# A fused attention and GEGLU block: all engines in written order in the FFN, attention in eight pieces, LayerNorm sums from the residual add and a Square

## The chip, the cores and the metric

The kernel runs on one core of a Trainium2 chip. The metric is the device time of one execution in microseconds (us). Every figure for a kernel is the median of several executions unless it is said to be of one profiled execution; the span in a profile is some 1.7 us shorter than the time of the same execution. A run is called slow when it is over 1.5% above the fastest of the same kernel; one execution of one experiment was, and it is left out. The granted clock is the share of TensorE's full clock that the profile records; at 0.50, half clock.

Names of engines in the profile: PE is TensorE (matmul), PEld its weight loads, DVE VectorE, ACT ScalarE, POOL GpSimd, SP SyncE, which issues most transfers. An L with a number is a line of that kernel's own text, so the same statement has slightly different numbers in different kernels.

## The reference

2048 tokens of width 640, bf16; 32 heads of width 20; FFN width 1536.

```python
def _A_ref(x, wqkv, w_phi, wo):            # linear attention, H = 32, Dh = 20
    q, k, v = ...                          # x @ wqkv, split into heads
    pq = jnp.einsum("bhsd,hdf->bhsf", q, w_phi)
    pk = jnp.einsum("bhsd,hdf->bhsf", k, w_phi)
    phi_q = jnp.concatenate([_softmax(pq), _softmax(-pq)], axis=-1)
    phi_k = jnp.concatenate([_softmax(pk), _softmax(-pk)], axis=-1)
    kv = jnp.einsum("bhsf,bhsd->bhfd", phi_k, v)
    z = jnp.einsum("bhsf->bhf", phi_k)
    num = jnp.einsum("bhqf,bhfd->bhqd", phi_q, kv)
    den = jnp.einsum("bhqf,bhf->bhq", phi_q, z)[..., None] + 1e-6
    return merge_heads(num / den) @ wo     # (shortened)

def _B_ref(x, w_gate, w_up, w_down):
    return (_gelu(x @ w_gate) * (x @ w_up)) @ w_down

h  = x + _A_ref(_layernorm(x), A_wqkv, A_w_phi, A_wo)
h2 = h + _B_ref(_layernorm(h), B_w_gate, B_w_up, B_w_down)
```

## The kernel before

It has three stages. *Statistics*: for each of 16 tiles of 128 tokens LN1, a transpose, the value and key projections (pv, pk; w_phi is folded into the key and query weights beforehand), and the sums kvp. *Queries*: the query projection pq of all tiles, and attention of the first tiles. *FFN*: gate and up projection (gu), gelu, product GT, down projection (pd); attention of the later tiles is woven between these units. A unit of the FFN is one gate_up or one down call. Cut to what the change and the argument touch:

```python
    ctx.enter_context(tc.manual_schedule(engines={nc.tensor.engine, nc.sync.engine}))   # written order, to the end
    man_cm = tc.manual_schedule()                 # written order on all engines ...
    man_cm.__enter__()
    ...
    def ln_stats(pool, tiles, tag, act=True):
        ...
            for i in range(2):
                nc.vector.bn_stats(stats[:, i, :], xt[:, i * HD:(i + 1) * HD])
            nc.vector.bn_aggr(mv[:, j, :], stats)
        nc.gpsimd.tensor_scalar_add(ve, mv[:, :, 1], EPS)
        nc.gpsimd.tensor_tensor(rstd, ve, nhalf[:, 0:n], op=ALU.pow)
        if act:
            nc.gpsimd.tensor_tensor(mr, mv[:, :, 0], rstd, op=ALU.mult)
            nc.gpsimd.tensor_scalar_mul(mr, mr, -1.0)
    ...
    for t in range(NT):                           # statistics
        k_tile(t)
        ...
        if t == 12:
            fold(WqT, Wq2)                        # casts of wa: alternately ScalarE and VectorE
        if t + 3 < NT:
            v_tile(t + 3)
        if 6 <= t + 5 < NT:
            ln_ap(t + 5, on_act=True)             # normalise on ScalarE, then transpose by DMA
        k_norm(t)                                 # sk, rs on VectorE; vt on GpSimd and VectorE
        if t % 2 == 1 and t + 7 < NT:
            ln_st(t + 7, t + 8)                   # LN1 statistics
        if t % 2 == 1 and t >= 5:
            kv_tile(t - 5)
            kv_tile(t - 4)
    ...
    def attn_a(t): ...                            # ab matmuls, AB on ScalarE
    def attn_b(t):                                # pr, den, rd: VectorE
        ...
    def attn_b2(t, on_pe=False):                  # w, tt, o: VectorE; transpose of o by DMA
        ...
    def attn_c(t): ...                            # po matmuls
    def attn_d(t, act=True):                      # residual add, LN2 statistics
        ht = x_sb[t // 4][:, t % 4, :]
        h2 = ht.rearrange("p (u f) -> p u f", u=2)
        nc.vector.tensor_tensor(h2, st[t][:, :, 0:HD], h2, ALU.add)
        st[t] = ln_stats(p2, [ht], "2", act)[0]
    def attn_e(t): ...                            # LN2 applied on ScalarE, transpose by DMA
    ...
    man_cm.__exit__(None, None, None)             # ... until here; the scheduler orders DVE, ACT, POOL from now on

    def attn_at(t, i, start=0, slow=2, sep=0):    # at which unit which piece is written
        pcs = [(i, attn_a, t), (i + 1, attn_b, t), (i + 1 + sep, attn_b2, t),
               (i + 3 + slow, attn_c, t), (i + 4 + slow, attn_d, t), (i + 5 + slow, attn_e, t)]
        ...
    weave(gus(0, 0, 256) + downs(0, (0, 1)), ...)           # first pass, half-width units
    weave(gus(0, 256, 512) + downs(0, (2, 3)), ...)         # second
    for b in range(1, NB):                                  # blocks 1, 2, 3
        ...
```

The softmax here doesn't subtract the row's maximum and nothing guards it: scores larger than these inputs give would overflow.

## Time and profile before

| | before |
|---|---|
| time, median of the first 3 executions | 297.85 us (296.56 to 298.58) |
| span of the profiled execution | 298.0 us |
| TensorE busy | 94% |
| VectorE, ScalarE, GpSimd busy | 64%, 45%, 26% |
| stretch from first pk to first gu | 84.3 us |
| stretch from first gu to last pd matmul | 192.8 us |

The last two rows are differences of start times in the timeline of TensorE. As TensorE is busy almost throughout, such a stretch is its work plus its stops, and it doesn't move with what happened before it.

### The profile page before, as it was taken

Reading aid. Unit: us, or ns where it says so; the run is one execution under the profiler, and the core shown is the slowest. Engines: PE = TensorE matmul, PEld = TensorE weight load, DVE = VectorE, ACT = ScalarE, POOL = GpSimd, SP = SyncE. Lnnn points to the kernel's source line nnn. Section 1 sums busy time; section 2 is a strip of 40 time slices with the busy share of each in tenths; the row PEclk is TensorE's granted clock in tenths of the full one; section 3 lists DMA queues with packets and bytes.
Section 4 is the critical chain, followed back from the end, with each engine's and each line's share of the span. In section 5 each row is a group of like instructions: output and inputs, shape, how many; then the busy total and the mean of one; then the engine's idle time right before and its main releaser. Section 6 shows DMA issues by size and latency. Waiting matters only on the chain.

```text
span 298.0 us, 5561 instructions
## 1 busy us (share of the span) xinstructions
PE 280.7 (94%) x2233; PEld 179.8 (60%) x2233; DVE 189.7 (64%) x370; ACT 133.0 (45%) x200; POOL 77.7 (26%) x138
## 2 busy tenths in 40 slices
PE   6799699989999899799999998999998999999995
PEld 2576477765555678477876554577554567544473
DVE  4799979878276599574755868643777753232322
ACT  1479768866968846234242443410534321122200
POOL 5439877855221101311110033110002321000000
PEclk9999989999999999989999999999999999999999
DMA  7995312381080021513112112221111422100011
GB/s 216 263 343 167 54 23 50 65 311 66 2 264 2 0 25 34 56 45 77 35 25 66 23 24 46 44 60 52 46 22 22 45 46 68 44 0 0 2 41 47
DMA packets 40968, 21.01 MB, mean 71 GB/s; under 512 B 33136, under 2 KB 39280, under 8 KB 40944
## 3 DMA queue, kind: packets, MB, share of 16 engines
q1 hardware_dynamic: 39712, 19.50, 26.6%
q10 hardware_dynamic: 1232, 1.17, 1.2%
q8 instruction: 17, 0.28, 0.4%
q14 instruction: 7, 0.06, 0.1%
HBM read 10.18 MB, written 2.62 MB: 43 GB/s over the span
## 4 chain that ended last, share of the span: by engine, by line
PE 69%; DVE 9%; issue 8%; POOL 6%; DMA 4%; ACT 3%; ACTq 0%; POOLq 0%
PE gu L479 28%; PE pd L494 15%; PE pq L309 7%; PE pk L236 5%; PE po L459 5%; PE pv L236 4%; DVE stats L100 3%; PE ab L408 2%; PE kvp L281 2%; POOL rstd L105 2%; POOL vt L270 1%; DMA LN1T<-ln 1%; DMA x_sb<-in_A_x_dram 1%; DMA oT<-o 1%; DVE x_sb L467 1%
## 5 line engine op out<-in xcount | busy, mean ns | idle before, releaser
L479 PE MATMUL gu<-LN2T,Wg 128*128 128x512 bf16 (+1 forms) x300 | 61.7, 336 | 2.1 <-DVE GT L485 1.5
L479 PE MATMUL gu<-LN2T,Wu 128*128 128x512 bf16 (+1 forms) x300 | 61.7, 336 | 0.0
L485 DVE TENSOR_TENSOR GT<-gu,g 128x512 bf16<-128x512 f32 (+1 forms) x60 | 34.2, 577 | 38.2 <-ACT g L482 38.1
L482 ACT ACTIVATE g<-gu 128x512 bf16<-128x512 f32 (+1 forms) x60 | 29.5, 507 | 59.0 <-PE gu L479 57.5
L494 PE MATMUL pd<-Wd,GT 128*128 128x320 bf16 x384 | 53.6, 299 | 2.1 <-DVE GT L485 2.1
L494 PEld LDWEIGHTS <-GT 128*128 128x128 bf16 x384 | 37.5, 98 | 17.3 <-DVE GT L485 2.9
L103 POOL TENSOR_SCALAR ve<-mv 128x1 f32<-128x1 f32 (+1 forms) x26 | 5.9, 226 | 145.1 <-DVE mv L101 140.1
L479 PEld LDWEIGHTS <-Wg 128*128 128x128 bf16 x300 | 29.0, 98 | 23.2 <-issue 2.7
L479 PEld LDWEIGHTS <-Wu 128*128 128x128 bf16 x300 | 29.3, 98 | 22.6
L236 PEld LDWEIGHTS <-LN1T 128*128 128x128 bf16 x320 | 30.9, 99 | 15.8 <-DMA LN1T<-ln 3.3
L115 ACT ACTIVATE ln<-x_sb,mr,rstd 128x640 bf16<-128x640 bf16 x24 | 22.2, 923 | 37.4 <-POOL mr L110 37.4
L270 POOL TENSOR_TENSOR vt<-vS,rs 128x672 bf16<-128x672 bf16 x22 | 32.9, 1507 | 13.1 <-DVE rs L267 13.1
L500 DVE TENSOR_TENSOR y<-pd,x_sb 128x640 bf16<-128x640 f32 (+1 forms) x17 | 13.3, 782 | 30.2 <-PE pd L494 30.2
L100 DVE BATCH_NORM_STATS2 stats<-x_sb 128x6 f32<-128x320 bf16 x64 | 27.7, 474 | 2.6 <-DMA x_sb<-in_A_x_dram 2.1
L236 PE MATMUL pv<-Wv,LN1T 128*128 128x320 bf16 x160 | 25.1, 306 | 2.8 <-DMA LN1T<-ln 2.4
L413 ACT COPY AB<-ab 128x968 f32<-128x968 f32 x16 | 15.4, 966 | 25.9 <-PE ab L408 25.9
L459 PE MATMUL po<-Wo,oT 128*128 128x320 bf16 x160 | 25.5, 308 | 0.7 <-DVE GT L485 0.4
L265 DVE TENSOR_REDUCE sk<-E 128x64 f32<-128x1280 bf16 x16 | 23.6, 1472 | 3.4 <-ACT E L259 3.4
L440 DVE TENSOR_TENSOR tt<-AB,w 128x1280 bf16<-128x1280 f32 x16 | 23.9, 1492 | 0.6
L236 PE MATMUL pk<-Wk,LN1T 128*128 128x320 bf16 x160 | 24.2, 299 | 0.0
L259 ACT ACTIVATE E<-pk 128x640 bf16<-128x640 f32 x32 | 20.7, 703 | 7.0 <-PE pk L236 7.0
L309 PE MATMUL pq<-LN1T,Wq 128*128 128x512 bf16 x100 | 22.9, 379 | 0.4 <-ACT Eq L314 0.4
(63 smaller groups left out, 258.3 us busy)
## 6 DMA issues: line engine op xcount, KB each, us to landing
out_dram<-y SPq DMA_DIRECT2D x15, 160.0 KB, 1.8
Wg<-in_B_w_gate_dram SPq DMA_DIRECT2D x1, 1920.0 KB, 11.8
Wu<-in_B_w_up_dram SPq DMA_DIRECT2D x1, 1920.0 KB, 9.3
Wd<-in_B_w_down_dram SPq DMA_DIRECT2D x1, 1920.0 KB, 8.0
x_sb<-in_A_x_dram SPq DMA_DIRECT2D x2, 640.0 KB, 5.5
Wv<-in_A_wqkv_dram SPq DMA_DIRECT2D x2, 400.0 KB, 5.8
Wo<-in_A_wo_dram SPq DMA_DIRECT2D x1, 800.0 KB, 5.1
x_sb<-in_A_x_dram ACTq DMA_DIRECT2D x1, 640.0 KB, 6.8
```

The source lines that it names most:

```text
L100: nc.vector.bn_stats(stats[:, i, :], xt[:, i * HD:(i + 1) * HD])
L115: nc.scalar.activation(ln, xt, ACTF.Identity, bias=mr, scale=rstd)
L236: nc.tensor.matmul(ps[:, u, 0:HD], lhsT=lnT(t, c), rhs=W[:, c, u * HD:(u + 1) * HD], start=(c == 0), stop=(c == NC - 1))
L265: nc.vector.reduce_sum(sk, Ek[t].rearrange("p s (h f) -> p (s h) f", f=Dh), axis=AX.X)
L270: eng.tensor_tensor(vt[:, s], vS[t % 6], rs[:, s * H:(s + 1) * H, None].to_broadcast([P, H, VC]), ALU.mult)
L309: nc.tensor.matmul(pqs[j][:, i, :], lhsT=Wq2[:, kc, c * P:(c + 1) * P], rhs=LN1T[b][:, kc, :], start=(kc == 0), stop=(kc == NC - 1))
L440: nc.vector.tensor_tensor(tt.rearrange("p s (h f) -> p s h f", f=Dh), num, w[:, :, :, None].to_broadcast([P, 2, H, Dh]), ALU.mult)
L459: nc.tensor.matmul(po[:, u, 0:HD], lhsT=st[t][:, c, :], rhs=Wo[:, c, u * HD:(u + 1) * HD], start=(c == 0), stop=(c == NC - 1))
L479: nc.tensor.matmul(gu[:, i, 0:n], lhsT=W[:, c, f * P:(f + 1) * P], rhs=LN2T[b][:, c, a0:a1], start=(c == 0), stop=(c == NC - 1))
L482: nc.scalar.activation(g[:, 0:n], gu[:, 0, 0:n], ACTF.Gelu_apprx_tanh)
L485: nc.vector.tensor_tensor(st[b, "g", f][:, a0:a1], gu[:, 1, 0:n], g[:, 0:n], ALU.mult)
L494: nc.tensor.matmul(pd[:, u, 0:HD], lhsT=st[b, "g", f][:, tl * P:(tl + 1) * P], rhs=Wd[:, f, u * HD:(u + 1) * HD], start=(f == 0), stop=(f ...
```

## The change

Four intents. (1) In the FFN, too, VectorE, ScalarE and GpSimd follow the written order, and attention is cut into eight pieces at new offsets, so that no piece stands ahead of work that is ready. (2) VectorE is relieved: small products of attention go to GpSimd, and LN2's mean and variance come from the residual add's accumulator and a Square on ScalarE in place of bn_stats. (3) At the start and in the statistics the LN1 work is moved up. (4) Loads are reordered and output stores issued three units later. The diff, cut to its core (cuts marked with an ellipsis):

```diff
@@ ln_stats, small operation @@
-            nc.gpsimd.tensor_tensor(mr, mv[:, :, 0], rstd, op=ALU.mult)
-            nc.gpsimd.tensor_scalar_mul(mr, mr, -1.0)
+            for j in range(n):
+                nc.gpsimd.tensor_scalar(mr[:, j:j + 1], mv[:, j, 0:1], rstd[:, j:j + 1], -1.0, ...)
@@ loads: first tiles of x and w_phi change places and queues @@
+    nc.scalar.dma_start(wphi, ...)
     nc.sync.dma_start(x_sb[0][:, 0:1, :], x_v[:, 0:1, :])
-    nc.scalar.dma_start(x_sb[0][:, 1:2, :], x_v[:, 1:2, :])
+    nc.sync.dma_start(x_sb[0][:, 1:2, :], x_v[:, 1:2, :])
...
@@ start: third tile's statistics earlier, mask product BD from GpSimd to VectorE @@
+    ln_st(2, act=False)
     ln_ap(1, on_pe=True)
...
-    nc.gpsimd.tensor_tensor(BD, ...)
...
+    nc.vector.tensor_tensor(BD, ...)
@@ statistics @@
-        k_norm(t)
         if t % 2 == 1 and t + 7 < NT:
             ln_st(t + 7, t + 8)
+        k_norm(t)
@@ attention: b, b2, b3 (pr, den | rd, w | tt, o); eng is GpSimd in the FFN @@
-        nc.vector.tensor_tensor(pr, ...)
+        eng.tensor_tensor(pr, ...)
...
@@ attn_d, and a new attn_d2 @@
+        nc.vector.scalar_tensor_tensor(h2, st[t][:, :, 0:HD], 1.0, h2, op0=ALU.mult, op1=ALU.add, accum_out=sm[:, 0:1])
...
+        nc.scalar.activation(sq, ht, ACTF.Square, accum_out=sm[:, 1:2])
+        ...                                      # four one-column operations and a pow on GpSimd: rstd and -mean*rstd
@@ FFN @@
-    man_cm.__exit__(None, None, None)            # before the FFN
+    SHORT = (0, 2, 3, 4, 9, 9, 10, 12)           # offsets of the eight pieces, in units
+    LONG = (0, 1, 2, 3, 6, 6, 7, 8)
...
+    man_cm.__exit__(None, None, None)            # after it
```

More of the change, by code (lines that the diff above doesn't have):

```diff
@@ L108, in ln_stats @@
         if act:
-            nc.gpsimd.tensor_tensor(mr, mv[:, :, 0], rstd, op=ALU.mult)
-            nc.gpsimd.tensor_scalar_mul(mr, mr, -1.0)
+            for j in range(n):
+                nc.gpsimd.tensor_scalar(mr[:, j:j + 1], mv[:, j, 0:1], rstd[:, j:j + 1], -1.0,
+                                        op0=ALU.mult, op1=ALU.mult)
         return [(xt, mv[:, j, 0:1], rstd[:, j:j + 1], mr[:, j:j + 1]) for j, xt in enumerate(tiles)]
@@ L147 @@
     WqT = p1.tile([P, NC, D], BF16, name="WqT")
+    nc.scalar.dma_start(wphi, phi_v.rearrange("(c p) f -> p c f", p=P))
     nc.sync.dma_start(x_sb[0][:, 0:1, :], x_v[:, 0:1, :])
-    nc.scalar.dma_start(x_sb[0][:, 1:2, :], x_v[:, 1:2, :])
+    nc.sync.dma_start(x_sb[0][:, 1:2, :], x_v[:, 1:2, :])
     for u in range(2):
         nc.sync.dma_start(Wv[:, :, u * HD:(u + 1) * HD], w_v[:, :, 2 * D + u * HD:2 * D + (u + 1) * HD])
-        if u == 0:
-            nc.scalar.dma_start(x_sb[0][:, 2:3, :], x_v[:, 2:3, :])
-            nc.scalar.dma_start(wphi, phi_v.rearrange("(c p) f -> p c f", p=P))
-    nc.scalar.dma_start(x_sb[0][:, 3:4, :], x_v[:, 3:4, :])
+        nc.scalar.dma_start(x_sb[0][:, 2 + u:3 + u, :], x_v[:, 2 + u:3 + u, :])
     nc.sync.dma_start_transpose(WkT, A_wqkv[:, D:2 * D])
@@ L323 @@
     warm(2)
-    ln_st(2, act=False)
-    nc.gpsimd.tensor_tensor(BD, wphi[:, :, None, :].to_broadcast([P, NC, 8, Dh]),
-                            hmask[:, :, :, None].to_broadcast([P, NC, 8, Dh]), ALU.mult)
     v_mm(0, (0,))
@@ L335 @@
     v_ev(1)
+    nc.vector.tensor_tensor(BD, wphi[:, :, None, :].to_broadcast([P, NC, 8, Dh]),
+                            hmask[:, :, :, None].to_broadcast([P, NC, 8, Dh]), ALU.mult)
     ln_st(3, act=False)
@@ L419, in attn_a, with attn_b, attn_b2, attn_b3 @@
         st[t] = AB
-    def attn_b(t):
+    def attn_b(t, on_pe=False):
+        eng = nc.vector if on_pe else nc.gpsimd
         AB = st[t]
         pr = small(p2, [P, H, 2], "pr", 2)
-        nc.vector.tensor_tensor(pr, AB[:, 0, :, Dh:KC], AB[:, 1, :, 0:KC:KC - 1], ALU.mult)
+        eng.tensor_tensor(pr, AB[:, 0, :, Dh:KC], AB[:, 1, :, 0:KC:KC - 1], ALU.mult)
         den = small(p2, [P, H], "den", 2)
-        nc.vector.tensor_tensor(den, pr[:, :, 0], pr[:, :, 1], ALU.add)
+        eng.tensor_tensor(den, pr[:, :, 0], pr[:, :, 1], ALU.add)
+        st[t] = AB, den
+    def attn_b2(t, on_pe=False):
+        eng = nc.vector if on_pe else nc.gpsimd
+        AB, den = st[t]
         rd = small(p2, [P, H], "rd", 2)
         nc.vector.reciprocal(rd, den)
-        st[t] = AB, rd
-    def attn_b2(t, on_pe=False):
-        AB, rd = st[t]
         w = small(p2, [P, 2, H], "w", 2)
         for s in range(2):
-            nc.vector.tensor_tensor(w[:, s], AB[:, 1 - s, :, s * (KC - 1)], rd, ALU.mult)
+            eng.tensor_tensor(w[:, s], AB[:, 1 - s, :, s * (KC - 1)], rd, ALU.mult)
+        st[t] = AB, w
+    def attn_b3(t, on_pe=False):
+        AB, w = st[t]
         tt = p2.tile([P, 2, D], BF16, name="tt", bufs=2)
@@ L466, in attn_d, with attn_d2 @@
         h2 = ht.rearrange("p (u f) -> p u f", u=2)
-        nc.vector.tensor_tensor(h2, st[t][:, :, 0:HD], h2, ALU.add)
-        st[t] = ln_stats(p2, [ht], "2", act)[0]
+        if not act:
+            nc.vector.tensor_tensor(h2, st[t][:, :, 0:HD], h2, ALU.add)
+            st[t] = ln_stats(p2, [ht], "2", False)[0]
+            return
+        sm = small(p2, [P, 2], "sm", 2)
+        nc.vector.scalar_tensor_tensor(h2, st[t][:, :, 0:HD], 1.0, h2, op0=ALU.mult, op1=ALU.add, accum_out=sm[:, 0:1])
+        st[t] = sm
+    def attn_d2(t):
+        sm = st[t]
+        ht = x_sb[t // 4][:, t % 4, :]
+        sq = p2.tile([P, D], BF16, name="sq", bufs=1)
+        nc.scalar.activation(sq, ht, ACTF.Square, accum_out=sm[:, 1:2])
+        v = small(p2, [P, 3], "v2", 2)
+        nc.gpsimd.tensor_scalar(v[:, 0:1], sm[:, 0:1], sm[:, 0:1], -1.0 / (D * D), op0=ALU.mult, op1=ALU.mult)
+        nc.gpsimd.tensor_scalar_add(v[:, 0:1], v[:, 0:1], EPS)
+        nc.gpsimd.tensor_scalar(v[:, 1:2], sm[:, 1:2], 1.0 / D, v[:, 0:1], op0=ALU.mult, op1=ALU.add)
+        rstd = small(p2, [P, 1], "rstd2")
+        nc.gpsimd.tensor_tensor(rstd, v[:, 1:2], nhalf[:, 0:1], op=ALU.pow)
+        nc.gpsimd.tensor_scalar(v[:, 2:3], sm[:, 0:1], rstd, -1.0 / D, op0=ALU.mult, op1=ALU.mult)
+        st[t] = ht, None, rstd, v[:, 2:3]
     def attn_e(t, on_pe=False, on_dve=False):
@@ L488, in down @@
         if u == 0:
-            st["pd"] = gtile("pd"), p2.tile([P, D], BF16, name="y", bufs=3)
+            st["pd"] = gtile("pd"), p2.tile([P, D], BF16, name="y", bufs=4)
         pd, y = st["pd"]
@@ L501, in down, with store @@
                                     x_sb[b][:, tl, :].rearrange("p (u f) -> p u f", u=2)[:, a:u + 1], ALU.add)
-            nc.sync.dma_start(o_v[:, 4 * b + tl, a * HD:(u + 1) * HD], y[:, a * HD:(u + 1) * HD])
-    later = []
+            stores.append((lag, o_v[:, 4 * b + tl, a * HD:(u + 1) * HD], y[:, a * HD:(u + 1) * HD]))
+            if b == NB - 1 and tl >= 2:
+                store(lag)
+    later, stores, lag = [], [], 3
+    def store(n):
+        stores[:] = [(i - n, *x) for i, *x in stores]
+        while stores and stores[0][0] <= 0:
+            _, dst, src = stores.pop(0)
+            nc.sync.dma_start(dst, src)
     def weave(units, stages):
@@ L513, in weave @@
                 g(*a)
+            store(1)
             fn(*args)
@@ L527 @@
     q_mm(q + 1)
-    attn_b(0)
+    attn_b(0, True)
     attn_b2(0, True)
+    attn_b3(0, True)
     attn_a(1, True)
@@ L535 @@
     q_mm(q + 3)
-    attn_b(1)
+    attn_b(1, True)
     attn_b2(1, True)
+    attn_b3(1, True)
     attn_c(0)
@@ L552, with attn_at @@
     attn_e(1, True, True)
-    man_cm.__exit__(None, None, None)
     assert q + 6 == len(Eq)
-    def attn_at(t, i, start=0, slow=2, sep=0):
-        pcs = [(i, attn_a, t), (i + 1, attn_b, t), (i + 1 + sep, attn_b2, t), (i + 3 + slow, attn_c, t), (i + 4 + slow, attn_d, t), (i + 5 + slow, attn_e, t)]
-        return pcs if start == 0 else pcs[start:]
+    def attn_at(t, i, offs):
+        fns = (attn_a, attn_b, attn_b2, attn_b3, attn_c, attn_d, attn_d2, attn_e)
+        return [(i + o, fn, t) for fn, o in zip(fns, offs) if o >= 0]
+    SHORT = (0, 2, 3, 4, 9, 9, 10, 12)
+    LONG = (0, 1, 2, 3, 6, 6, 7, 8)
     weave(gus(0, 0, 256) + downs(0, (0, 1)),
-          attn_at(2, 0, 1, 3, 1) + attn_at(3, 3, 0, 3, 1) + attn_at(4, 6, 0, 4) + attn_at(5, 9, 0, 4) + attn_at(6, 13, 0, 4))
-    weave(gus(0, 256, 512) + downs(0, (2, 3)), attn_at(7, 3, 0, 4))
+          attn_at(2, 0, (-1, 0, 1, 2, 7, 7, 8, 10)) + attn_at(3, 1, SHORT) + attn_at(4, 6, SHORT) + attn_at(5, 9, SHORT) +
+          attn_at(6, 13, SHORT))
+    weave(gus(0, 256, 512) + downs(0, (2, 3)), attn_at(7, 2, SHORT))
     for b in range(1, NB):
@@ L568 @@
             for tl in range(4):
-                stages += attn_at(4 * b + 4 + tl, (0, 2, 5, 7)[tl])
+                stages += attn_at(4 * b + 4 + tl, (0, 2, 5, 7)[tl], LONG)
         weave(gus(b, 0, 512) + downs(b, range(4)), stages)
+    man_cm.__exit__(None, None, None)
 _INS = ['A_x', 'A_wqkv', 'A_w_phi', 'A_wo', 'B_x', 'B_w_gate', 'B_w_up', 'B_w_down']
```

## The prediction

> **What bounds the kernel now.** I read the page first, then the chain of waits, then the timeline of TensorE, then all engines around each hole in it.
>
> ```profile
> PE 280.7 (94%) x2233; PEld 179.8 (60%) x2233; DVE 189.7 (64%) x370; ACT 133.0 (45%) x200; POOL 77.7 (26%) x138
> ...
> PEclk9999989999999999989999999999999999999999
> ```
>
> TensorE is the bound in every stage; VectorE is dense only in the first 60 us. The second line shows two dents in the granted clock. How fast TensorE can go is read from the chain, where nothing else interferes:
>
> ```profile
> 194.59 13.04 PE pd L494 x96
> ...
> 255.92 25.90 PE gu L479 x120
> ```
>
> That is 0.136 us for 320 columns and 0.216 us for 512, start to start. With such a floor for every width (columns at 2.4 GHz plus 2.5 ns; 0.022 us for the half-array matmuls that make kvp) I summed over the whole timeline the distance from each start to the next less the floor. Floor 270.0 us, lost 23.4 us, first start at 1.25 us, 3.36 us after the last start: together 298.0. The change removes no matmul, so it can only win inside the 23.4. By stretch: 0 to 20 us 6.3; 20 to 40 us 4.6; 40 to 100 us 2.3 (mostly the query fold at 61 to 63 us); 100 to 132 us 6.7; 140 to 150 us 1.0; around 180 us 1.1; around 228 us 1.1. The big ones:
>
> ```profile
> 11.66 0.45 PE L128 MATMUL tp<-ident,ln 128*128 128x128 bf16 x5 [1.43 <-DVE ln L120]
> ...
> 36.08 2.39 PE L236 MATMUL pv<-Wv,LN1T 128*128 128x320 bf16 x10 [2.41 <-DMA LN1T<-ln]
> ```
>
> Behind the first: a GpSimd mask product and a VectorE normalisation that start together, the latter then taking 1.64 us where its neighbours take 0.45:
>
> ```profile
> 9.89 1.52 POOL L326 TENSOR_TENSOR BD<-wphi,hmask 128x800 bf16<-128x800 bf16 x1
> 9.97 1.64 DVE L120 TENSOR_SCALAR ln<-x_sb,mv,rstd 128x640 bf16<-128x640 bf16 x1 [1.00 <-POOL rstd L105]
> ```
>
> Behind the second: GpSimd does two vt products before the small LayerNorm operations that ScalarE needs:
>
> ```profile
> 26.52 2.59 POOL L270 TENSOR_TENSOR vt<-vS,rs 128x672 bf16<-128x672 bf16 x2
> 29.20 0.22 POOL L103 TENSOR_SCALAR ve<-mv 128x2 f32<-128x2 f32 x1
> ...
> 30.86 0.92 ACT L115 ACTIVATE ln<-x_sb,mr,rstd 128x640 bf16<-128x640 bf16 x1 [0.49 <-POOL mr L110]
> ```
>
> The hole in the first FFN pass, all engines:
>
> ```profile
> 120.95 1.49 DVE L440 TENSOR_TENSOR tt<-AB,w 128x1280 bf16<-128x1280 f32 x1
> ...
> 121.03 1.50 POOL L110 TENSOR_SCALAR mr<-mr 128x1 f32<-128x1 f32 x1
> 121.09 1.52 PE L494 MATMUL pd<-Wd,GT 128*128 128x320 bf16 x10
> 122.57 0.92 ACT L115 ACTIVATE ln<-x_sb,mr,rstd 128x640 bf16<-128x640 bf16 x1 [3.08 <-POOL mr L110]
> 123.39 0.64 ACT L482 ACTIVATE g<-gu 128x256 bf16<-128x256 f32 x2
> ...
> 124.27 0.31 PE L494 MATMUL pd<-Wd,GT 128*128 128x320 bf16 x1 [1.66 <-DVE GT L485]
> ```
>
> The scheduler put the normalisation on ScalarE ahead of two gelus whose inputs were ready; it waits for a one-column GpSimd operation that takes 1.50 us instead of 0.24 because tt runs; TensorE waits for the gelus. The same triple (tt, mr of 1.41 us, ln ahead of gelu) stands at 176 to 178 us and again 48 us later.
>
> Both long holes are followed by half clock:
>
> ```profile
> 36.58:40.00 3.42, 3.42 (x49) 2.28 (x48) 3.32 (x5) 1.45 (x2) 2.50 (x3) 0.50 0.00 0
> ...
> 125.33:128.75 3.42, 3.42 (x23) 2.35 (x22) 0.84 (x2) 0.00 (x0) 0.00 (x0) 0.50 0.50 96
> ```
>
> **What the Trainium skill says.** (1) "TensorE: Matmul & The Clock Gate", section "What's actually happening": the gate judges a free-running window of 3413 ns and halves the clock after an idle one. The trace agrees on the length, not on "idle": both windows before were still about a third busy. The hole at 9.9 to 11.7 us cost no clock. (2) The same page, "Wait - 56ns, not 53.3ns?": N / 2.4 GHz plus 2.5 ns per matmul; the chain rows agree (135.8 and 215.8 ns). (3) "SBUF — State Buffer", "Who interferes with whom": a VectorE instruction with two SBUF inputs, or in a two-port mode, and a GpSimd one that reads SBUF exclude each other for a whole instruction. Agreed: 1.50 against 0.24, 1.64 against 0.45. (4) "ScalarE: Activation LUTs", "What ACT_TABLE_LOAD costs": an ACTIVATE with immediates is 186 ns + 0.833 ns a column, and a switch of table costs a load (1.28 us here, twice in the kernel). Square on 640 columns: 0.72 us by that; the 640-column PSUM copies here take 0.70.
>
> **The change part by part.**
>
> *Start.* The mask product goes to VectorE (800 elements; the 672-element product there takes 0.86, so about 1.0 us) behind the third tile's normalisation, whose statistics move up. By hand from the durations: second tile's transpose 0.4 us later; third tile's statistics end near 7.9, rstd near 8.8, its normalisation at 9.3; TensorE reaches its transpose at 10.4 without a stop, against 11.66. The key fold then meets WkT, which landed at 13.4 us, and VectorE's copies of it come about a microsecond earlier. First key projection 16.5 instead of 17.6: **-1.0**. The reordered loads keep the first tile first; I count nothing for them.
>
> *Statistics before k_norm.* On GpSimd the rstd and mr of tiles 8, 9 end near 28.5 instead of 30.8, so ln of tile 8 becomes limited by ScalarE's own order, 0.6 us earlier. The transpose then took 4.2 us where most take 2.6, with an instruction fetch of 1.2 us on one DMA engine inside it. Without a collision the stop of 2.57 almost vanishes, with one about 1.8 stay. I take **-1.5**. VectorE falls further behind on k_norm, but kvp takes those four to five tiles later. Half clock behind it: 10 matmuls lose 0.13 each, about 1.4; at three in four that it goes, **-1.1**.
>
> *Work moved off VectorE.* For each of 14 tiles pr 0.23, den 0.19, w 0.35, two statistics 0.89, aggregate 0.21: 1.9 us, 26 us in all. Added: Square on ScalarE, 14 x 0.72 = 10 us (45% busy); on GpSimd four operations on 32 to 64 columns (0.25 to 0.3 by its 84-column rows at 0.33) and four one-column ones plus the power 0.57: about 2.5 us a tile in place of 1.25. All of it is beside TensorE; it counts through order only.
>
> *Written order, first pass.* Lost there: 0.54 + 0.12 + 0.43 + 0.18 + 1.82 + 0.60 and 1.05 of half clock = 4.7. By hand with the new offsets: the table load delays the first gelu as now, so with tile 3's attn_a at unit 1, unit 2 waits 0.35 for a PSUM buffer; tt and o of tiles 2 and 3 come before GT of units 2 and 5 on VectorE, so the first po waits about 1.1 for GT of unit 5; 0.15 elsewhere. The last gelu now comes before a Square, not behind a blocked ln: GT 11 lands just as the down projection asks for it. New loss 1.6: **-3.1**.
>
> *Second half-pass and blocks 1, 2.* Lost 0.59 + 0.43, then 1.1 twice. With 2.16 us units and ln emitted a unit after its GpSimd chain, I find no stop; I leave 0.2 in each: **-0.8** and **-1.8**. The late stores only keep transposes from queueing behind them: 0. The last 45 us are unchanged.
>
> Sum: 1.0 + 1.5 + 1.1 + 3.1 + 0.8 + 1.8 = 9.3, so 288.5. Fourteen tiles get three new hand-overs each between VectorE and GpSimd; I give 0.8 back for one or two I overlooked: **289.3**.
>
> **Rivals.** (a) *The small GpSimd operations become the new wait*: tt (two SBUF inputs) locks GpSimd 1.4 us at a time, and rd stands in VectorE's queue ahead of GT. For: the 1.50 us above. Against: each piece now sits a unit or more (1.1 or 2.2 us) apart. If half the tiles lose 0.4, the FFN gain shrinks by 3: 292. (b) *The transpose stays the limit at 33 us and the clock drops anyway*: 2.5 back, 291.8. (c) *Square forces table loads*: two of 1.28 us per tile would push the time over 310. Against: Copy and Identity run between gelus with no load, and the page says cheap functions sit in every set, though it doesn't name Square there; 3%. (d) *Everything fits*, the fold and first-pass waits shrink too: 286.
>
> **Range and chances.** (a) and (b) together give 294, (d) 286; runs before spread over 2 us. So 289.3, 286.0 to 293.5. Faster by 2% means below 292.0: 0.83; within 2%: 0.15; slower: 0.02.
>
> **What would show it.** The third transpose starts without a stop near 10.4; the first pk near 16.5; pv's wait for LN1T falls under 1.8; no 0.50 clock after the first 10 us; VectorE falls by about 25 us, GpSimd rises by 10 to 20; no ln waits over a microsecond ahead of a gelu; two table loads still. Wrong if TensorE's waits for GT in the first pass exceed 2 us, if a half-clock window returns, or if GpSimd ends TensorE's waits by way of rd.

## More of the kernel before

The chain of waits of the kernel before over the statistics (15 to 63 us), summed by line and cut off by the view at its width, reads:

```profile
by line: PE pk L236 23.9%; PE pv L236 22.0%; POOL vt L270 9.0%; DMA LN1T<-ln 8.8%; PE kvp L281 8.7%; ACT E L259 5.5%; POOL KV L355 3.1%; DVE sk L265 3.1%; ACT Wq L209 2.6%; ACT ln L115 1.9%; issue 1.6%; DVE stats L100 1.6%; POOL rstd L105 1
```

It runs through TensorE's own matmuls. VectorE (sk, stats) has 5% of it.

## The result, and the profile after

| | before | after |
|---|---|---|
| time, median of 4 executions each | 297.74 us (296.56 to 298.58) | 290.37 us (290.09 to 290.75) |
| ratio, 95% interval | | 0.9756 (0.9721 to 0.9792) |
| span of the profiled execution | 298.0 us | 288.6 us |
| first pk starts at | 17.59 us | 16.66 us |
| first pk to first gu | 84.30 us | 82.59 us |
| first gu to last pd matmul | 192.76 us | 186.00 us |

A ratio here is the mean time of one kernel's fast runs over the mean of the other's in the same rounds, so it isn't quite the ratio of the medians. The time fell by 7.4 us, inside the predicted range and 1.1 us above its middle.

The engines and the clock, from the page of the kernel after:

```profile
PE 275.7 (96%) x2218; PEld 177.4 (61%) x2233; DVE 167.7 (58%) x287; ACT 144.2 (50%) x228; POOL 99.1 (34%) x207
...
PEclk9999999999999999999999999999999999999999
```

VectorE has lost 22 us and 83 instructions (predicted: about 25 us), GpSimd has gained 21 us (10 to 20), ScalarE 11 us. No slice of the clock is below 9 tenths. (The profile holds 2218 of 2233 matmul records; the kernel issues the same number as before.)

The start, from TensorE's timeline of the kernel after (columns: start, duration, engine, line, operation, output<-inputs, count, and in brackets idle time before it and what ended it):

```profile
8.99 1.52 PE L235 MATMUL pv<-Wv,LN1T 128*128 128x320 bf16 x10 [0.81 <-DMA Wv<-in_A_wqkv_dram]
...
10.35 0.44 PE L129 MATMUL tp<-ident,ln 128*128 128x128 bf16 x5
...
14.01 1.12 PE L202 MATMUL wa<-BD,WkT 128*128 128x140 bf16 x18 [0.50 <-DMA WkT<-in_A_wqkv_dram]
...
16.66 1.52 PE L235 MATMUL pk<-Wk,LN1T 128*128 128x320 bf16 x10 [0.19 <-DVE Wk L210]
```

The third transpose starts at 10.35 us without a stop (predicted: near 10.4), but the value projection before it now waits 0.81 us for its weights, and the key fold 0.50 us for WkT. The first pk comes at 16.66 us (predicted: 16.5). The two waits for the transposed LN1 in the statistics, and the normalisation behind the second:

```profile
28.09 1.53 PE L235 MATMUL pv<-Wv,LN1T 128*128 128x320 bf16 x10 [1.20 <-DMA LN1T<-ln]
...
30.29 0.92 ACT L116 ACTIVATE ln<-x_sb,mr,rstd 128x640 bf16<-128x640 bf16 x1
...
34.95 1.53 PE L235 MATMUL pv<-Wv,LN1T 128*128 128x320 bf16 x10 [1.25 <-DMA LN1T<-ln]
```

The wait at tile 8 fell from 2.41 to 1.25 us, to below the predicted 1.8; but at tile 6, where the kernel before loses 0.41 us from start to start, 1.36 us are lost now (the 1.20 us of the line and the matmul's own start). In the trace the transfer of tile 6 was issued at 24.54 us and landed at 28.04; it took 3.5 us where an undisturbed one takes 2.57; the load of Wg landed at 27.42. In the kernel before, the same transfer landed at 28.02. What the start had won was waited for here. It repeats: in the kernel after, s_start, a_dve, a_bn, a_store, a_ctl, a_small and a_ln this transfer was issued at 23.65 to 25.53 us and landed 0.57 to 0.63 us after Wg each time.

The chain of waits over the statistics of the kernel after (15 to 61 us), by line, again cut off by the view:

```profile
by line: DVE sk L264 35.9%; DVE vt L269 15.7%; DVE rs L266 14.6%; DVE stats L100 13.6%; DVE mv L101 3.6%; PE pk L235 3.3%; issue 2.9%; ACT E L258 2.8%; PE wa L202 2.8%; DVE Wk L210 1.8%; ACT Wk L208 1.5%; DVE Wq L210 1.5%; DVEq L266 0.4%; P
```

VectorE's sk, vt, rs and stats now hold four fifths of it. Before it was TensorE. The prediction did not foresee this. Being on the chain is not yet a cost: the query fold of this kernel waits for VectorE only 0.2 us. What it can cost, s_lnst and a_best below show.

The FFN's hand-over at the end of the first pass, where the kernel before waited 1.66 us behind a blocked ln, from the timeline of the kernel after:

```profile
116.37 1.49 DVE L445 TENSOR_TENSOR tt<-AB,w 128x1280 bf16<-128x1280 f32 x1
...
116.55 1.44 POOL L487 TENSOR_SCALAR v<-sm 128x1 f32<-128x1 f32 x1 [1.01 <-DVE x_sb L478]
116.71 0.38 ACT L507 ACTIVATE g<-gu 128x256 bf16<-128x256 f32 x1 [1.20 <-PE gu L504]
...
116.99 0.73 ACT L485 ACTIVATE sq<-x_sb 128x640 bf16<-128x640 bf16 x1
...
117.60 1.81 PE L519 MATMUL pd<-Wd,GT 128*128 128x320 bf16 x12
...
117.86 0.38 ACT L507 ACTIVATE g<-gu 128x256 bf16<-128x256 f32 x1
...
119.89 0.92 ACT L116 ACTIVATE ln<-x_sb,v,rstd 128x640 bf16<-128x640 bf16 x1 [1.65 <-POOL v L492]
```

The same collision is still there: tt runs, and the one-column GpSimd operation beside it takes 1.44 us (as do four of the fourteen of its kind; the other ten take 0.27). But the ln that needs it is written after both gelus and after the Square, and ScalarE idles for 1.65 us with nothing to do, while TensorE goes from gu to pd without a stop.

The new and moved small operations, from the groups of the kernel after (columns: line, engine, operation, tile, shapes, count, busy us, mean ns, idle us before):

```profile
L487 POOL TENSOR_SCALAR v<-sm 128x1 f32<-128x1 f32 x14 | 8.4, 602 | 31.3 <-DVE x_sb L478 31.3
...
L425 POOL TENSOR_TENSOR pr<-AB 128x64 f32<-128x64 f32 x14 | 7.0, 501 | 22.8 <-ACT AB L415 22.8
L438 POOL TENSOR_TENSOR w<-AB,rd 128x32 f32<-128x32 f32 x28 | 6.8, 264 | 22.6 <-DVE rd L434 22.6
```

```profile
L485 ACT ACTIVATE sq<-x_sb 128x640 bf16<-128x640 bf16 x14 | 10.2, 730 | 4.2 <-DVE x_sb L478 4.2
...
L485 ACT ACTIVATION_READ_ACCUMULATOR sq<-x_sb 128x1 f32 x14 | 2.7, 191 | 0.0
```

The Square takes 0.73 us as predicted, and reading its accumulator another 0.19, which the prediction had left out. There are still two table loads of 1.28 us.

### The profile page after: what moved, and what is told of

The parts are those of the page before. It is cut to its first block, busy times and chain, and to the rows that moved or that the text cites. A ratio compares the mean times of both kernels' runs of the same rounds, so it can differ in the third digit from the quotient of the medians.

```text
span 288.6 us, 5553 instructions
## 1 busy us (share of the span) xinstructions
PE 275.7 (96%) x2218; PEld 177.4 (61%) x2233; DVE 167.7 (58%) x287; ACT 144.2 (50%) x228; POOL 99.1 (34%) x207
## 4 chain that ended last, share of the span: by engine, by line
PE 73%; DVE 15%; DMA 6%; ACT 3%; issue 1%; POOL 1%; DVEq 0%; ACTq 0%; POOLq 0%
PE gu L504 33%; PE pd L519 18%; PE pq L308 8%; PE po L464 7%; DVE sk L264 6%; DMA WkT<-in_A_wqkv_dram 4%; PE ab L407 3%; DVE vt L269 3%; DVE rs L266 2%; DVE stats L100 2%; PE pk L235 2%; DMA oT<-o 1%; ACT Eq L313 1%; DMA wphi<-in_A_w_phi_dram 1%; PE wa L202 1%
## 5 line engine op out<-in xcount | busy, mean ns | idle before, releaser
L507 ACT ACTIVATE g<-gu 128x512 bf16<-128x512 f32 (+1 forms) x60 | 30.7, 512 | 74.9 <-PE gu L504 69.8
L269 POOL TENSOR_TENSOR vt<-vS,rs 128x672 bf16<-128x672 bf16 x22 | 34.5, 1591 | 8.9 <-DVE rs L266 6.3
L235 PE MATMUL pv<-Wv,LN1T 128*128 128x320 bf16 x160 | 24.2, 299 | 3.3 <-DMA LN1T<-ln 2.5
L464 PE MATMUL po<-Wo,oT 128*128 128x320 bf16 x160 | 24.4, 299 | 0.4 <-DMA oT<-o 0.4
L313 ACT ACTIVATE Eq<-pq 128x1024 bf16<-128x1024 f32 x20 | 19.4, 1025 | 3.4 <-PE pq L308 3.4
L464 PEld LDWEIGHTS <-oT 128*128 128x128 bf16 x160 | 15.5, 98 | 8.0 <-DMA oT<-o 1.2
L487 POOL TENSOR_SCALAR v<-sm 128x1 f32<-128x1 f32 x14 | 8.4, 602 | 31.3 <-DVE x_sb L478 31.3
```

The lines of the kernel that those rows point to most:

```text
L235: nc.tensor.matmul(ps[:, u, 0:HD], lhsT=lnT(t, c), rhs=W[:, c, u * HD:(u + 1) * HD], start=(c == 0), stop=(c == NC - 1))
L269: eng.tensor_tensor(vt[:, s], vS[t % 6], rs[:, s * H:(s + 1) * H, None].to_broadcast([P, H, VC]), ALU.mult)
L313: nc.scalar.activation(Eq[j][:, :, s, :], pqs[j], ACTF.Exp, scale=(1.0, -1.0)[s])
L464: nc.tensor.matmul(po[:, u, 0:HD], lhsT=st[t][:, c, :], rhs=Wo[:, c, u * HD:(u + 1) * HD], start=(c == 0), stop=(c == NC - 1))
L507: nc.scalar.activation(g[:, 0:n], gu[:, 0, 0:n], ACTF.Gelu_apprx_tanh)
```

## The experiments

Three chips (6, 0 and 10), each with its own runs of the kernel before. I read four things of each kernel: the time, the two stretches of the profiled execution, and the mean granted clock of every execution. Under "clock" a half-clock window means a stretch of 3.41 us at 0.50 inside the kernel (windows in the last 3 us are left out). All runs gave a correct result.

| kernel | time, us | ratio (95%) | first pk | first pk to first gu | first gu to last pd | half-clock windows, start |
|---|---|---|---|---|---|---|
| before | 296.3 / 298.1 / 298.2 | 1 | 17.59 | 84.30 | 192.76 | 36.6, 125.3 |
| after | 290.37 | 0.9756 | 16.66 | 82.59 | 186.00 | none |
| s_start | 296.23 | 0.9977 (0.9904-1.0051) | 16.54 | 82.36 | 191.28 | none |
| s_lnst | 297.43 | 1.0011 (0.9956-1.0065) | 17.38 | 84.21 | 191.37 | 61.7 |
| f_only | 291.04 | 0.9802 (0.9754-0.985) | 17.14 | 82.91 | 185.89 | none |
| f_order | 317.98 | 1.0718 (1.0661-1.0775) | 17.23 | 84.31 | 212.85 | 35.4 and six later |
| a_sched | 312.81 | 1.0487 (1.0428-1.0545) | 17.53 | 82.57 | 207.38 | four, from 125.2 |
| a_dve | 294.45 | 0.9864 (0.9825-0.9903) | 17.01 | 82.65 | 190.25 | none |
| a_bn | 294.26 | 0.986 (0.9818-0.9901) | 15.92 | 82.59 | 190.32 | none |
| a_store | 290.63 | 0.9732 (0.9683-0.9781) | 16.57 | 82.54 | 186.15 | none |
| a_ctl | 291.56 | 0.9787 (0.975-0.9824) | 17.66 | 82.57 | 186.03 | none |
| a_small | 292.39 | 0.9804 (0.9768-0.984) | 17.30 | 83.08 | 186.98 | none |
| a_ln | 290.79 | 0.9773 (0.9731-0.9816) | 16.38 | 82.70 | 186.00 | none |
| a_best | 291.41 | 0.9776 (0.9736-0.9817) | 16.87 | 84.24 | 186.27 | 56.2 |

The three times of before are the medians on chips 6, 0 and 10; s_start to f_order ran on chip 6, a_sched to a_store on chip 0, the last four on chip 10. Compare ratios, not times, across chips.

"Lost" is, as in the prediction, the distance from one matmul's start to the next less the floor; the idle time in the brackets of a profile line is some 0.15 us shorter.

The stretch of the FFN separates kernels far better than the time: among five kernels with the same FFN code (after, a_ctl, a_ln, a_best, f_only) it lies between 185.89 and 186.27 us. The start is the contrary: the ten kernels with the new start code have their first pk between 15.92 and 17.66 us (mean 16.84), the four with the old one between 17.14 and 17.59 (mean 17.34). The kernel after and a_ctl, which are the same program, differ there by 1.00 us, so no single first pk shows the start's worth.

My theory after reading the result was that the new order of the FFN is worth most and the rest little. The rivals were that the gain comes from the start and the statistics, from the relief of VectorE alone, or from the half clock alone.

### s_start: the kernel before with the new start alone

```diff
+ loads, earlier ln_st(2) and BD on VectorE as in the change; the rest of the kernel before
```

> The kernel before with the start alone changed: the rearranged loads, the third tile's statistics moved up, the mask product on VectorE. My account: first key projection about 0.9 us earlier than 17.6 us, but the end only 0 to 1 us earlier (296.7 to 297.7), because the transposed LN1T of tile 6 cannot land before the big load of Wg does (27.4 us) and TensorE gives the time back as a longer wait for LN1T. Rival: the start's 0.9 us arrives at the end in full, and more if the half clock near 37 us goes (295.5).

Measured: 0.9977 (one of its four executions was slow and is not in it). First pk at 16.54 us, as predicted; but at tile 6 1.23 us are lost for LN1T, where the kernel before loses 0.41, and at tile 8 1.29 us (before: 2.57) although its statistics are in the old order. The prediction's term for the statistics was sized from this second wait, and it shrank with the start alone. So start and statistics are not two gains that add, and neither shows in the time. The FFN's stops are those of before: 1.81 us at 119.5 us and 0.79 us at 175.6 and 223.9.

### s_lnst: the kernel before with LN1's statistics ahead of k_norm alone

```diff
-        k_norm(t)
         if t % 2 == 1 and t + 7 < NT:
             ln_st(t + 7, t + 8)
+        k_norm(t)
```

> The kernel before with only the order of k_norm and the statistics of tiles t+7, t+8 swapped. My account: GpSimd has mr of tiles 8 and 9 some 2 us earlier, TensorE's wait of 2.57 us at 33.7 us falls to about 1.5 and the half-clock window behind it goes: 2 to 3 us gained (294.7 to 295.7). Rival: ScalarE's own order and the transpose decide, wait and half clock stay: within 0.7 us of before.

Measured: 1.0011. The wait at tile 8 fell from 2.57 to 1.37 us lost, and the total did not move (2 to 3 us were expected). The ln of tile 8 started 0.78 us earlier (30.08 in place of 30.86 us), as the mechanism says; the rest is a transfer that took 3.61 us in place of 4.23, which the edit doesn't explain. Where it went, the query fold of this kernel shows (timeline):

```profile
59.22 0.47 PE L203 MATMUL wa<-BD,WqT 128*128 128x140 bf16 x6 [0.76 <-ACT E L259]
...
59.99 0.76 DVE L211 CAST Wq<-wa 128x640 bf16<-128x640 f32 x1
...
60.80 0.79 PE L203 MATMUL wa<-BD,WqT 128*128 128x140 bf16 x12 [1.10 <-DVE Wq L211]
```

TensorE waits 1.10 us for VectorE's cast of Wq (in the kernel before the longest wait there is 0.76 us, for ScalarE). VectorE has done the statistics first and is late by most of what TensorE has gained; the fold's casts stand in its queue behind sk, rs and vt, and hand the delay back: 0.31 us lost at the fold's second stop in the kernel before, 1.27 here. This is one profile; in the kernels with the whole change this stop loses from under 0.25 to 0.90 us, in the kernel after 0.32. In three of four executions a half-clock window remained (clock 0.994), in the profiled one behind this very stop, at 61.7 us.

### f_only: the change without its start, loads and statistics order

```diff
  FFN as in the change; loads, start, order of k_norm and the two mr operations as in the kernel before
```

> The changed kernel with start, loads and the order of k_norm put back: only the FFN's part of the change. My account: the FFN's part is worth about 5.5 us (4.7 + 1.0 + 1.1 + 1.1 lost before, 1.6 left over): 292 to 292.5, with the half clock near 37 us still there and the one near 127 us gone. Rival, that most of the gain came from the first 40 us: 295 or more.

Measured: 0.9802, all four executions at clock 1.00. The FFN takes 185.89 us, as in the kernel after. In the profiled one the stop at tile 8 is there (2.43 us lost) and no half clock follows it, against the expectation. So the change of the FFN alone brings most of the whole; what start and statistics add is under 1% and not resolved here.

### f_order: the kernel before in written order to the end, with the old pieces

```diff
-    man_cm.__exit__(None, None, None)
     ...
+    man_cm.__exit__(None, None, None)            # after the last weave
```

> The kernel before with all engines in written order to the end, nothing else: old offsets, old work on VectorE. My account: written order alone is not enough, since ln stands one unit (1.1 us) behind statistics and a GpSimd chain of 2.5 us or more, so gelus wait behind ln in the first pass as before or worse: 296 to 301. Rival, that the scheduler's order was the whole loss: 293 or less.

Measured: 1.0718, or 318 us where 296 to 301 were expected: the direction was right, the size far off. The FFN is 21.5 us slower than in s_start and s_lnst, six half-clock windows among it. One of its longest stops, all engines:

```profile
190.35 1.49 DVE L440 TENSOR_TENSOR tt<-AB,w 128x1280 bf16<-128x1280 f32 x1
190.51 1.42 POOL L110 TENSOR_SCALAR mr<-mr 128x1 f32<-128x1 f32 x1
...
191.97 0.92 ACT L115 ACTIVATE ln<-x_sb,mr,rstd 128x640 bf16<-128x640 bf16 x1 [3.28 <-POOL mr L110]
...
192.79 0.94 ACT L413 COPY AB<-ab 128x968 f32<-128x968 f32 x1
...
193.79 1.44 PE L479 MATMUL gu<-LN2T,Wg 128*128 128x512 bf16 x3 [3.68 <-ACT AB L413]
```

Written order makes it certain that the AB copy stands behind the ln, the ln behind mr, and mr beside tt: 3.68 us. The kernel before has fewer and shorter ones of these. Written order is no gain by itself; it only does what the offsets say.

### a_sched: the change with the scheduler ordering VectorE, ScalarE and GpSimd in the FFN

```diff
+    man_cm.__exit__(None, None, None)            # before the FFN, as in the kernel before
     ...
-    man_cm.__exit__(None, None, None)
```

> The changed kernel, but the FFN's VectorE, ScalarE and GpSimd order left to the scheduler again (TensorE and the DMA queue stay in written order): same operations, same offsets. If the gain is the order (ln no longer ahead of gelus, no tt between a GT and its reader): most of the FFN's 5 us is lost again, ratio to before 0.993 or more (294 us and up). If the gain is the work taken off VectorE: stays at 0.98.

Measured: 1.0487. New pieces, small operations and sums are all there, and the FFN is 21 us slower than in the kernel after. One of its stops:

```profile
195.24 0.74 ACT L485 ACTIVATE sq<-x_sb 128x640 bf16<-128x640 bf16 x1 [1.67 <-DVE x_sb L478]
...
197.57 0.92 ACT L116 ACTIVATE ln<-x_sb,v,rstd 128x640 bf16<-128x640 bf16 x1 [1.50 <-POOL v L492]
198.40 0.57 ACT L507 ACTIVATE g<-gu 128x512 bf16<-128x512 f32 x1
...
199.00 0.69 DVE L510 TENSOR_TENSOR GT<-gu,g 128x512 bf16<-128x512 f32 x1 [3.85 <-ACT g L507]
...
199.75 0.31 PE L519 MATMUL pd<-Wd,GT 128*128 128x320 bf16 x1 [3.80 <-DVE GT L510]
```

The Square stands ahead of a gelu and waits for the residual add; then ln stands ahead of it and waits 1.50 us for the last of the GpSimd operations. VectorE waits 3.85 us for that gelu, and pd starts 3.80 us late. The longer chain over three engines needs the written order more than the old one did. In this kernel order and offsets are worth something only together.

### a_dve: the change with small products and LN2 statistics back on VectorE

```diff
-        eng = nc.vector if on_pe else nc.gpsimd
+        eng = nc.vector
...
-        nc.vector.scalar_tensor_tensor(h2, ..., accum_out=sm[:, 0:1])
+        nc.vector.tensor_tensor(h2, st[t][:, :, 0:HD], h2, ALU.add)
+        st[t] = ln_stats(p2, [ht], "2", act)[0]              # attn_d2 empty
```

> The changed kernel with pr, den, w and the LN2 statistics back on VectorE (bn_stats, no Square), in the new written order with the new offsets. If order and offsets carry the gain: 1 to 3 us above the changed kernel, in the first pass, where VectorE then has some 30 us of work for 26 us of TensorE's (ratio 0.978 to 0.987). If the lighter VectorE carries it: back at before or worse (0.995 and up).

Measured: 0.9864, the FFN 190.25 us: 4.25 us over the kernel after, 1.1 us under the kernel before without half clock there (191.3 in s_start and s_lnst). The ratio lies in the range expected if order and offsets carry the gain (0.978 to 0.987), but in the stretch of the FFN they bring, without the rest, only these 1.1 us of 5.3.

### a_bn: the same with the small products left on GpSimd

```diff
  only attn_d and attn_d2 as in the run before
```

> The changed kernel with LN2 statistics alone back on VectorE (bn_stats after the residual add), the small attention operations still on GpSimd. 1.1 us more on VectorE a tile, inside the slack of the new offsets: 0 to 1 us above the changed kernel (ratio 0.975 to 0.982).

Measured: 0.986, the FFN 190.32 us, the same as a_dve; the expected 0 to 1 us was missed by over 3. So with LN2's sums undone it makes no difference where the small products are. How bn_stats costs TensorE time, around 130 us:

```profile
126.92 0.21 DVE L101 BATCH_NORM_AGGREGATE mv<-stats 128x2 f32<-128x12 f32 x1
...
127.22 0.22 POOL L103 TENSOR_SCALAR ve<-mv 128x1 f32<-128x1 f32 x1 [6.08 <-DVE mv L101]
...
128.42 0.37 POOL L425 TENSOR_TENSOR pr<-AB 128x64 f32<-128x64 f32 x1
...
129.13 0.35 DVE L434 RECIPROCAL rd<-den 128x32 f32<-128x32 f32 x1 [1.32 <-POOL den L427]
...
130.08 1.49 DVE L445 TENSOR_TENSOR tt<-AB,w 128x1280 bf16<-128x1280 f32 x1 [0.32 <-POOL w L438]
...
132.49 0.71 PE L505 MATMUL gu<-LN2T,Wg 128*128 128x256 bf16 x5 [1.52 <-DVE GT L511]
```

On GpSimd ve, the first operation behind the statistics, waits 6.08 us until VectorE has done residual add, two bn_stats and the aggregate; pr and den of the next tile stand behind it, though their input AB was complete at 121.78 us. VectorE then idles 1.32 us at rd for den, with a GT behind it whose gelu was done at 128.30; tt comes next, and the GT after tt is the one that TensorE waits 1.52 us for. In the kernel after, pr and den were written and done before, rd does not wait, and TensorE's wait there is 0.27 us. This run can't say how much of the 4.3 us is the length of bn_stats and how much the place of its GpSimd operations a unit earlier than in the change: other offsets for bn_stats were not tried. GpSimd's queue can't be the only way, for a_dve costs the same with pr and den on VectorE.

### a_store: the change with stores at once

```diff
-            if b == NB - 1 and tl >= 2:
-                store(lag)
+            store(lag)                                       # and 3 buffers for y again
```

> The changed kernel with the output stores issued at once and three y buffers, as before. My account: the late stores are worth nothing to half a microsecond (a transpose behind a store waits at most for y, about 1 us, inside its slack): ratio 0.974 to 0.978. Rival: transposes queued behind stores make TensorE wait for oT or LN2T: 1 us or more.

Measured: 0.9732, FFN 186.15 us. Late stores bring nothing.

### a_ctl: the changed kernel again, as a control on the third chip

No edit.

> The changed kernel itself, unaltered, as a control for the three beside it. Expected: a ratio of 0.974 to 0.978 to the kernel before, about 290.4 us, every execution at a granted clock of 1.0. If executions of it with a half-clock window turned up, the theory that the new order has removed those windows for good would fall.

Measured: 0.9787, a little above the expected 0.974 to 0.978. Five of six executions were at clock 0.998 or 1.00 (290.56 to 291.84 us); one had 0.994 and took 292.96. So the theory that the new order has removed half-clock windows for good falls: they have become fewer, not impossible. Of 25 executions of the kernel before on the three chips, 7 were at 0.998 or above; of the changed kernel's ten, nine.

### a_small: the change with pr, den and w back on VectorE, LN2's sums kept

```diff
-        eng = nc.vector if on_pe else nc.gpsimd
+        eng = nc.vector
```

> The changed kernel with the small operations of attention (pr, den, w) put back from GpSimd to VectorE; LN2's sums stay with the residual add and the Square. My theory: given the written order, the move to GpSimd is worth nearly nothing, so within 0.5 us of the control (ratio within 0.002 of it). Rival: it is these small operations that unload VectorE in attention, and the kernel is 1 us or more slower, with stops of over 0.5 us at gelu units.

Measured: 0.9804 against the control's 0.9787. The intervals overlap: by time it is within the 0.5 us expected (means of six executions 292.13 and 291.62). The stretches say more: the FFN is 0.95 us longer, with 0.45 us lost at 108.7 and 0.83 at 167.9 where the control loses under 0.3 and 0.56. So neither theory holds as stated. Beside the Square, moving the small products is worth about 1 us in the profiled FFN; beside bn_stats (a_bn against a_dve) it was worth nothing.

### a_ln: the change with LN1 applied ahead of the value projection's eviction

```diff
+        if 6 <= t + 5 < NT:
+            ln_ap(t + 5, on_act=True)
         if t + 3 < NT:
             v_tile(t + 3)
-        if 6 <= t + 5 < NT:
-            ln_ap(t + 5, on_act=True)
```

> The changed kernel with the LN1 application of tile t+5 written ahead of the value projection of tile t+3, so that it does not stand behind that tile's eviction on ScalarE. My theory: the start's gain is given back at the waits for LN1T, of which the one at tile 8 (1.25 us) is due to this order: that wait falls by 0.5 us or more, and the kernel is 0.5 to 1.5 us below the control. Rival: the transfer itself, behind the weight loads, sets the wait, and nothing is gained.

Measured: 0.9773, 0.8 us below the control by medians, with overlapping intervals: unclear. The wait at tile 8 has gone entirely. But:

```profile
28.77 1.53 PE L235 MATMUL pv<-Wv,LN1T 128*128 128x320 bf16 x10 [2.17 <-DMA LN1T<-ln]
```

```profile
58.74 0.47 PE L202 MATMUL wa<-BD,WqT 128*128 128x140 bf16 x6 [0.76 <-ACT E L258]
...
59.95 0.79 PE L202 MATMUL wa<-BD,WqT 128*128 128x140 bf16 x12 [0.73 <-DVE Wq L210]
```

Tile 6 now waits 2.17 us: its transfer, issued 0.9 us earlier than in the kernel after, landed only at 28.73 us, 0.57 us after Wg, so the loads seem to hold it (the next run tests this). And the fold waits 0.73 us for VectorE's Wq where the control waits 0.17. From first pk to first gu it takes 82.70 us against 82.57: what is gained at tile 8 is paid at tile 6 and at the fold.

### a_best: a_ln, with Wg loaded later and the query fold spread over five tiles

```diff
-    for dst, src in ((x_sb[2], ...), (x_sb[3], ...), (Wg, wg_v)):
+    for dst, src in ((x_sb[2], ...), (x_sb[3], ...)):
...
+        if 9 <= t < 9 + NC:
+            fold(WqT, Wq2, (t - 9,))                         # one part a tile
-        if t == 12:
-            fold(WqT, Wq2)
...
         if t == 10:
+            nc.sync.dma_start(Wg, wg_v)
```

> The changed kernel with the LN1 application moved as in the run before, the load of Wg moved from early in the statistics to the tenth tile, ahead of Wo and Wu, and the fold of Wq spread one part a tile over tiles 9 to 13. My theory: the transposed LN1 of tile 6 then no longer lands behind Wg (its wait of 1.20 us goes), and the stops of 0.92 and 0.32 us at the fold go too: 2.0 to 3.5 us below the control, about 287 us. Rival: Wg delays something later, or the transposes are late for another reason: within 0.5 us of the control.

Measured: 0.9776, no better than the control; a miss of 2 us. The first half worked: tile 6 no longer waits, its transfer takes 2.6 us. (Tile 8's takes 4.4 us and TensorE waits 1.22 us; what disturbed it is not settled.) The second half made it worse:

```profile
54.12 0.76 DVE L210 CAST Wq<-wa 128x640 bf16<-128x640 f32 x1
...
54.94 1.61 PE L235 MATMUL pk<-Wk,LN1T 128*128 128x320 bf16 x10 [2.48 <-DVE Wq L210]
...
56.95 2.85 PE L235 MATMUL pv<-Wv,LN1T 128*128 128x320 bf16 x10
```

The second cast of Wq on VectorE comes at 54.12 us, in the middle of its backlog, and TensorE waits 2.48 us; then a half-clock window starts at 56.2 us (ten matmuls of 320 columns take 2.85 us in place of 1.52). No version tried here beats the changed kernel beyond the noise. An obvious next one, all casts of the query fold on ScalarE, was not run.

## Why the prediction was right or wrong

The time was right, and so was the list of signs with small exceptions. The sum hid errors of both signs; that it came within 1.1 us of the result is in part luck.

**What bounds the kernel: right.** TensorE's floor is unchanged, and the gain came out of its stops.

**Start, -1.0: overestimated.** In the profile the first pk is 0.93 us earlier and the third transpose has no stop; that the 0.93 is so near the 1.0 is luck. Two things were not in the step. The first pk differs by up to 1.7 us between kernels with the same start code, and by 1.00 us between two profiles of the changed kernel, whose waits for loads ("I count nothing") differ: 0.98 us lost at Wv and 0.66 at WkT in the kernel after, 1.51 and 1.05 in a_ctl. The means of old and new start differ by 0.5 us (17.34 and 16.84). And the gain is partly waited for again at tile 6 behind the load of Wg (0.41 us lost before, 1.23 in s_start, 1.36 in the kernel after).

**Statistics before k_norm, -1.5: the failed step.** Alone the new order takes 1.20 us of loss from tile 8 (2.57 to 1.37 in s_lnst). Three things were wrong. First, the term doesn't add to the start's: s_start, with the old order, loses 1.29 us there, and the seven kernels with both and the change's place for ln lose 1.18 to 1.80. Second, what is won is waited for elsewhere: in the kernel after 0.95 us more are lost at tile 6, behind Wg. Third, the sentence "VectorE falls further behind on k_norm, but kvp takes those four to five tiles later" overlooks the query fold, whose casts stand in VectorE's queue: in s_lnst the fold pays back 0.95 us of the 1.20 (1.27 in place of 0.31 us lost at its second stop), and the chain of waits goes over to VectorE. In the kernel after the fold pays back nothing (0.32 us); its trace shows the first two only. From first pk to first gu f_only, with the old order, takes 82.91 us, the kernel after 82.59, and s_start, again with the old order, 82.36, all without a half-clock window: by these single profiles the order is worth between -0.2 and +0.3 us.

**Half clock, -1.1 here and 1.05 in the first pass: mis-sized, and mis-placed.** One profile decided this, and it held two windows. On chip 6 four executions of the kernel before without a window took 296.03 us on average, two with one (clock 0.994) 297.4, and one with two (0.989) 298.9: some 1.4 us each. The executions that the prediction is judged by averaged 297.66, and the window-free ones on chips 6, 0 and 10 were at 296.03, 296.77 and 296.2, near 296.3, so about 1.3 us of the 7.4 is clock, not 2.15. This is an estimate: the clocks of the executions that the prediction is judged by are not on record.

Where a window falls is partly luck, and the traces show it. In the profiles half clock begins and ends on a grid of 3.413 us (in the kernel before its two starts are 88.74 us apart, 26 times that), and the grid lies elsewhere in each of them. I cut TensorE's time along this grid in the twelve traces that record half clock (a_store and a_ln don't). Of the grid windows at full clock, twelve were followed by half clock inside the kernel: TensorE was busy for 6 to 45% of them. 974 were followed by full clock: the least busy had 46% (s_start, around the stop at 121.5 us), the next 51%. In the kernel before the stop at tile 8 lay in one grid window, which was 29% busy (1.00 of 3.41 us); in f_only the grid cut the same stop in two, with 72 and 62% (2.45 and 2.12 us), and no half clock followed. This is read from traces in which some matmul records are missing, and no run was made to test it; but by it the hole at tile 8 isn't bound to cost clock, as the prediction's term takes for granted, and four executions of f_only at full clock don't show that the hole is harmless.

**Written order and pieces in the FFN, -3.1, -0.8, -1.8: underestimated.** Without the half clock these are 2.05 + 0.8 + 1.8 = 4.65 us. Measured between the kernels before without a window in the FFN (191.28 and 191.37 in s_start and s_lnst) and after (186.00): 5.3 us. The term that was off is the left-over 1.6 us in the first pass, where only 0.43 us were lost (the foreseen wait of 0.35 for a buffer in PSUM, the memory that matmuls write to). The foreseen wait of 1.1 us of the first po for GT of unit 5 did not come, as po started at 108.72 us, before that GT ran at 109.47; I had taken the PSUM buffers for a strict rotation.

**Work off VectorE, "it counts through order only": right, but it hides a dependence.** Given the order and these offsets, bn_stats in place of the sums costs 4.3 us (a_bn); given the sums, the scheduler's order costs 21 us (a_sched); the order with the old pieces costs 21 us (f_order). Along one path the 5.3 us divide: order and offsets with the old work bring 1.1 us (a_dve), LN2's sums 3.3 more (a_small), the small products the last 1.0. Along another they divide otherwise (a_bn: the small products bring nothing without the sums). Not run were the scheduler's order with the old work at the new offsets, and the sums at the old offsets; nor were the cut into eight pieces and the offsets tried apart.

**Late stores, 0: right** (a_store).

**Rivals.** (a) small GpSimd operations as the new wait: not seen; their 1.44 us under tt ends ScalarE's idle time, not TensorE's. (b) half true: the transpose stays a limit with 1.25 us, and the clock does not follow. (c) false: two table loads. (d) false in the statistics. By the prediction's own terms (a) and (b) together give 294.8, not 294, and that lies above its range.

**The 0.8 us for things overlooked** was right by luck. It was meant for hand-overs between VectorE and GpSimd, and no wait of TensorE in the FFN is put down to GpSimd; the new waits are for loads: 0.81 us for Wv, 0.50 for WkT and 0.95 more lost at tile 6. In sum, as an estimate: start 0.5, statistics 0.3 at most, FFN 5.3, clock 1.3. That this gives the measured 7.4 us is no proof of the parts: only the FFN's 5.3 stands well clear of the spread of its stretch.

## What to carry to other kernels

In this kernel the written order lost 21 us with the old offsets, and the new pieces lost 21 us without the written order: try order and offsets as one change, and look for every operation of one engine that stands ahead of ready work of another. When a wait is taken from one stage, ask which queue has been made later by it and who reads that queue next; the view that shows it is the chain of waits of that stage, before and after. And read the granted clock of every execution, not of the profiled one alone, before counting on half-clock time.

## What the Trainium skill lacked or had wrong

- "TensorE: Matmul & The Clock Gate", section "What's actually happening", ties half clock to an idle window. Here twelve windows with TensorE busy for 6 to 45% were followed by half clock, and 974 with 46% or more were not. The page says that the window is free-running, which agrees: a stop of 2.43 us lost (f_only) was cut in two by the grid and brought no half clock, one of 2.57 (before) lay in one window and did. The busy share below which the clock is halved, and that one half-clock window costs about 1.4 us of this kernel, the page lacks.
- No page gives the time of reading an accumulator: 0.19 us each on ScalarE here and 0.083 us on VectorE, 14 times each. Nor was it said whether Square between gelus costs a table load: it brought no third one.
- "GPSIMD Engine Reference", section "Engine selection", puts GpSimd at about half of VectorE's speed for two-input element-wise operations. For the small ones here the ratio is smaller: 64 columns 0.37 against 0.23 us undisturbed (1.6 times), 32 columns 0.24 against 0.19 (1.3 times). With VectorE's tt beside them small GpSimd operations took up to 1.44 us, the one with one column 0.27 without.
- No page gives the latency of a small transpose by DMA from SBUF to SBUF beside loads: 2.57 us for 128 x 640 undisturbed; 3.1 to 5.1 us at tile 6 in eight kernels, where it landed 0.57 to 0.63 us after the load of Wg.
